# An attention-and-MLP block with gradients on one core: score matmuls of four heads on four 32-row strips from query chunk 1 on

## The chip, the core and the metric

The kernel runs on one core of a Trainium2 chip. The metric is the device time of one execution in microseconds (us); of several executions the median is given. Five engines work side by side: TensorE (PE in the profile, with its weight loads as PEld), VectorE (DVE), ScalarE (ACT), GpSimd (POOL) and SyncE (SP), which here only issues DMAs. TensorE writes into PSUM, which is handed out in banks of 128x512 f32.

## The reference

One adaLN block, forward and backward. 2048 tokens, width D = 512, 32 heads of 16 (DH), MLP width F = 1792:

```python
sa, ca, ga, sb, cb, gb = (silu(c) @ w_mod).reshape(6, D)
h = layernorm(x) * (1 + ca) + sa
q, k, v = heads(h @ wqkv)
p = softmax(q @ k.T * DH**-0.5)
x1 = x + ga * ((p @ v) @ wo)
h = layernorm(x1) * (1 + cb) + sb
out = x1 + gb * (relu(h @ w1 + b1)**2 @ w2 + b2)
```

The outputs are `out` and the gradients of all inputs for a given `grad_out`. Everything is bf16 in memory.

## The kernel before

The attention forward runs in `phase_fwd`. The 2048 queries are cut into 4 chunks (qc) of 512, the 32 heads into 8 groups (g) of four, and each group into two pairs (jp). A unit is one (qc, g, jp); in each unit a loop runs over 16 blocks (kb) of 128 keys. For one kb of one unit there are:

- two score matmuls (L388, 128x512) into the two banks of a tile `st`. The keys KTq hold four heads in four strips of 32 rows (16 rows of a head, the rest zero). Each matmul contracts over all 128 rows, and the queries `QTm0` to `QTm3` are zero outside the strip of their head, so one head's scores come out;
- one exponential on ScalarE over both (L391, 128x1024) into `pu`;
- eight value matmuls (L322, 128x17: 16 values and a column of ones that gives the softmax sum), which accumulate over kb in `accbank`, some blocks later. They wait in a list, `pend`, and a plan with a budget (SPAN, PVT) says how many go out in a block;
- `bg.step(1.14)`: a generator hands out a matmul or so of background work, which is the preparation of weights (`gen_weights`) and the MLP forward and part of the backward of the chunk before (`gen_mlp`: `x1`, `fc1`, `du`, `dx`, `fc2` and the output projection's gradient `gen_do`).

At a unit's end DVE normalises (L329 reciprocal, L330 multiply). `take_o` casts a finished chunk's output to bf16 and sends it through a DMA that transposes it for `gen_mlp`. Loads of the next unit's queries and of the next group's keys (`load_q`, `load_k`) stand on POOL's queue, at kb 1. PSUM's eight banks are: `st` 2 tiles of 2 banks, `accbank` 2, and `mps` 2 for the background. Within this code the orders on the engines TensorE, DVE, ScalarE and SP are written out by hand in chunk 0; from chunk 1 on TensorE and SP follow the order of the code, and a scheduler orders the rest.

Chunk 3 has no later forward to hide its MLP in: `last_chunk` does it after the last exponential (x1 at L817 and L818, layer norm L819 to L824, transposes `turn` L782 and L783, first matmul of fc1 at L838). There the rest of the background (`fc2` of chunk 2, L1255 to L1260) goes between these steps (`bg.take`, `bg.drain`). The attention backward, phase 5 of the trace (L1459 to L1659), is the longest part and isn't touched by the change.

Of the kernel before, what the change touches and what calls it, by code (L numbers as in the profile page):

```python
# [35 lines left out]
class Background:  # L36
# [27 lines left out]
    def step(self, rate):  # L64
# [4 lines left out]
        while self.gens and self.credit > 0:  # L69
# [36 lines left out]
class K:  # L106
# [22 lines left out]
    def dram(self, name, shape, dtype):  # L129
        if name in self.dbg:  # L130
            ap = self.dbg[name]
            assert tuple(ap.shape) == tuple(shape), (name, ap.shape, shape)
            return ap
        return self.dram_pool.tile(list(shape), dtype, name=name)

    def build(self, ctx: ExitStack):
        tc, nc = self.tc, self.nc
# [129 lines left out]
    def phase_fwd(self):  # L267
# [98 lines left out]
        late, self.late = self.late, None  # L366
        bg.until(-1)
        KT = self.KT_next
        for n, (qc, g, jp) in list(enumerate(order))[2:]:
            if (qc, g, jp) == (1, 0, 0):  # L370
                bg.drain()
                es.close()
                self.close_qkv()
                self.open_mlp()
                bg.add(self.gen_weights())
            accb = accp.tile([P, 512], F32, name="accbank")
            acc = accb[:, 0:8 * (DH + 1)].rearrange("p (a s e) -> p a s e", a=2, s=4)
            self.cur_g = g
            for kb in range(ST):
                if kb == (5 if qc == 0 and jp == 1 else 1) and n + 1 < len(order):  # L380
                    if n < 2 * NQ - 1 and jp == 1:
                        bg.until(g + 1)
                    load_q(*order[n + 1])
                    if jp == 1:
                        KTn = load_k(*order[n + 1][:2])
                stt = stp.tile([P, 2, 512], F32, name="st")
                for a in range(2):
                    nc.tensor.matmul(stt[:, a, :], lhsT=KT[:, kb * P:(kb + 1) * P], rhs=QTm[2 * jp + a][:],  # L388
                                     start=True, stop=True)
                pu = pup.tile([P, 2, 512], BF16, name="pu")  # L390
                nc.scalar.activation(pu[:], stt[:], ACT.Exp, scale=self.scale)  # L391
                u = (n, qc, g, jp, kb, acc, pu)
                now = n * ST + kb
                pend.extend((u, a, sub) for a in range(2) for sub in range(4))
                if late:
                    late.pop(0)()
                rate = 1.14 if qc else 1.2
                room = int((SPAN - 2 - bg.plan(rate)) / PVT)
                while pend:
                    age = now - max(pend[0][0][0] * ST + pend[0][0][4], 2 * ST - 2)  # L400
                    if age < 2 or (room <= 0 and age < 4):
                        break
                    pv(pend.pop(0))
                    room -= 1
                bg.step(rate)
            if jp == 1 and n + 1 < len(order):
# [12 lines left out]
        while pend:  # L419
            pv(pend.pop(0))  # L420
# [3 lines left out]
        self.last_chunk(bg, O_b, x0s, O32)  # L424

    def gen_open(self, Vaug, KT, QTm, QTo, stp, bg):

# [334 lines left out]
    def last_chunk(self, bg, O_b, x0s, o32):  # L762
# [51 lines left out]
        for k in range(4):  # L814
# [306 lines left out]
    def gen_weights_1(self):  # L1121
# [46 lines left out]
    def gen_mlp(self, sc, O_b):  # L1168
# [16 lines left out]
        for k in range(4):  # L1185
            x0 = mk.tile([P, D], BF16, name="x0", bufs=2)
            nc.gpsimd.dma_start(x0[:], x_v[:, k, :])
            pt = mps.tile([P, 512], F32, name="pps")
            for kt in range(DT):
                nc.tensor.matmul(pt[:], lhsT=OT[:, k, kt, :], rhs=self.wo[:, kt, :], start=(kt == 0), stop=(kt == DT - 1))  # L1190
# [18 lines left out]
        for ft in range(FT):  # L1209
            pt = mps.tile([P, 512], F32, name="pps")  # L1210
            for kt in range(DT):
                nc.tensor.matmul(pt[:], lhsT=self.w1[:, kt, ft * P:(ft + 1) * P], rhs=xhT[:, :, kt, :],
                                 start=(kt == 0), stop=(kt == DT - 1))
                yield 1
            nc.vector.tensor_scalar(rT[:, ft, :], pt[:], self.bias1[:, ft:ft + 1], 0.0, ALU.add, ALU.max)
# [4 lines left out]
        for ft in range(FT):  # L1220
            pt = mps.tile([P, 512], F32, name="pps")
            for kt in range(DT):
                nc.tensor.matmul(pt[:], lhsT=self.W2gbT[:, ft, kt, :], rhs=gT[:, kt, :], start=(kt == 0), stop=(kt == DT - 1))
# [8 lines left out]
        for k in range(4):  # L1232
# [1 line left out]
            nc.gpsimd.dma_start(gt[:], g_v[:, k, :])  # L1234
            pt = mps.tile([P, 512], F32, name="pps")
            for ft in range(FT):
                nc.tensor.matmul(pt[:], lhsT=duT[:, ft, k * P:(k + 1) * P], rhs=self.W1mT[:, :, ft, :],  # L1237
                                 start=(ft == 0), stop=(ft == FT - 1))
                yield 1
            dx1 = mk.tile([P, D], F32, name="dx1")  # L1240
# [6 lines left out]
            dxT = mk.tile([P, DT, P], BF16, name="dxT", bufs=2)  # L1247
            nc.sync.dma_start_transpose(dxT[:], dxb[:])
            todo.append((k, dxT))
            if k:  # L1250
                yield from self.gen_do(sc, *todo.pop(0))
        def fc2(k):
            pt = mps.tile([P, 512], F32, name="pps")
            for ft in range(FT):
                nc.tensor.matmul(pt[:], lhsT=rT[:, ft, k * P:(k + 1) * P], rhs=self.w2[:, ft, :], start=(ft == 0), stop=False)  # L1255
                yield 1
            nc.tensor.matmul(pt[:], lhsT=self.ones_b[0:1, :], rhs=self.b2gb_b[0:1, :], start=False, stop=True)
            yield 1
            o = mk.tile([P, D], BF16, name="o0", bufs=2)
            nc.vector.tensor_tensor(o[:], pt[:], x1[:, k, :], ALU.add)  # L1260
# [28 lines left out]
    def gen_do(self, sc, k, dxT, pads=None, o32=None):  # L1289
# [6 lines left out]
            nc.gpsimd.dma_start(o32, self.O32_d.rearrange("(st p) d -> p st d", p=P)[:, st, :])  # L1296
        pt = self.mps.tile([P, 512], F32, name="pps")
        for kt in range(DT):
            nc.tensor.matmul(pt[:], lhsT=dxT[:, kt, :], rhs=self.wogaT[:, :, kt, :], start=(kt == 0), stop=(kt == DT - 1))
# [666 lines left out]
```

## Time and profile before

| what | value |
|---|---|
| median of 3 executions | 2506.12 us (2504.64 to 2511.49) |
| span of the profiled execution | 2498.5 us, 7.6 us under the median of the timed runs |
| first exponential of chunk 1 starts | 272.24 us |
| last exponential of the forward ends | 980.54 us |
| first matmul of chunk 3's fc1 (L838) | 998.06 us |
| PE, ACT, DVE, POOL busy over the span | 96%, 91%, 68%, 30% |
| granted TensorE clock | 0.998 |

The span is the time from the first to the last instruction of the profiled execution; that execution has no other time of its own in what is shown, so all differences below are differences of spans. In a row of the timeline stand the start, the time from the first start to the last end of a run of like instructions, the engine, line, operation, tiles and the count (x), and in brackets how long the engine was idle before and what ended it. In a row of groups stand the count, the busy time, the mean time of one, and the idle time before them.

### The profile page before, as it was taken

The numbers are of one execution on the slowest core, as the hardware profiler recorded it, in microseconds if no ns is written. First come the engines' busy times: TensorE is split into PE (matmuls) and PEld (weight loads), VectorE is DVE, ScalarE is ACT, GpSimd is POOL, SyncE is SP. The second block draws the span as 40 slices with busy tenths as digits, with TensorE's granted clock in tenths as the row PEclk, the third lists the DMA queues.
The fourth block names the chain that finished last, engine by engine and source line by source line (L and its number), as shares of the span: only waits on it lengthen the run. The fifth ranks groups of instructions, "written<-read, shape, count | busy, mean of one in ns | idle before, by whom it ended". The sixth has DMA issues, their size and how long they took to land.

```text
span 2498.5 us, 67897 instructions
## 1 busy us (share of the span) xinstructions
PE 2410.2 (96%) x26211; PEld 1061.6 (42%) x26439; DVE 1695.0 (68%) x3487; ACT 2283.1 (91%) x3757; POOL 753.5 (30%) x1337
## 2 busy tenths in 40 slices
PE   8999999999999999999999999999999999999998
PEld 4555555555555555583233332333333333333343
DVE  6222322422332343576999999999999999999957
ACT  7999999999999997534999999999999999999945
POOL 2344531220131022245222323322333222322223
PEclk9999999999999999999999999999999999999999
DMA  4589661541243045499999999999999999999997
GB/s 166 135 179 208 169 125 47 132 100 40 92 114 98 23 123 147 110 199 216 232 235 233 232 227 231 237 234 231 230 235 239 234 230 236 234 233 236 238 217 192
DMA packets 1293547, 454.13 MB, mean 182 GB/s; under 512 B 1236948, under 2 KB 1261398, under 8 KB 1293222
## 3 DMA queue, kind: packets, MB, share of 16 engines
q1 hardware_dynamic: 1252422, 344.68, 71.8%
q0 software_dynamic: 38720, 104.04, 13.9%
q8 instruction: 207, 3.39, 0.6%
q10 hardware_dynamic: 2080, 1.05, 0.2%
q14 instruction: 118, 0.97, 0.1%
HBM read 75.83 MB, written 64.49 MB: 56 GB/s over the span
## 4 chain that ended last, share of the span: by engine, by line
PE 49%; ACT 35%; DMA 7%; issue 5%; DVE 3%; POOL 1%; SPq 1%; ACTq 0%; DVEq 0%; POOLq 0%
ACT pu L391 26%; PE st L1608 17%; PE acckv L1459 8%; ACT pu L1611 6%; DMA dsT<-ds 5%; PE accq L1484 5%; PE st L388 4%; PE dp L1522 2%; PE accbank L322 2%; PE dps L1050 2%; PE dp L1659 1%; PE st L1754 1%; ACT csq L1540 1%; PE pps L1237 1%; DVE ds L1526 1%
## 5 line engine op out<-in xcount | busy, mean ns | idle before, releaser
L1526 DVE TENSOR_TENSOR ds<-dp,pu 128x512 bf16<-128x512 f32 x1888 | 1166.0, 682 | 34.6 <-PE dp L1522 19.1
L1611 ACT ACTIVATE pu<-st 128x512 bf16<-128x512 f32 x2048 | 1073.8, 666 | 34.7 <-PE st L1608 21.3
L391 ACT ACTIVATE pu<-st 128x1024 bf16<-128x1024 f32 x992 | 912.1, 1077 | 4.2 <-PE st L388 3.7
L388 PE MATMUL st<-QTm,KTq 128*128 128x512 bf16 x1859 | 560.9, 377 | 27.1 <-ACT pu L391 6.1
L322 PEld LDWEIGHTS <-pu 128*128 128x128 bf16 x8192 | 346.7, 96 | 236.1 <-issue 3.0
L1522 PE MATMUL dp<-kvm,q 64*128 64x512 bf16 x1024 | 365.0, 384 | 2.0 <-DVE ds L1526 0.7
L322 PE MATMUL accbank<-Vaug,pu 128*128 128x17 bf16 x8192 | 357.4, 171 | 8.3 <-ACT Vaug L522 1.1
L1522 PE MATMUL dp<-kvm,dOTg 64*128 64x512 bf16 x1024 | 363.6, 383 | 0.3
L1608 PE MATMUL st<-kvm,q 64*128 64x512 bf16 x1024 | 349.4, 382 | 5.4 <-ACT pu L1611 0.2
L1608 PE MATMUL st<-kvm,QTg 64*128 64x512 bf16 x1024 | 348.1, 381 | 6.5
L1541 POOL TENSOR_TENSOR ds<-csq,pu 128x512 bf16<-128x512 f32 x128 | 147.2, 1150 | 627.0 <-ACT csq L1540 553.6
L388 PEld LDWEIGHTS <-KTq 128*128 128x128 bf16 x1984 | 188.4, 96 | 176.9 <-issue 124.8
L1459 PE MATMUL acckv<-ds,Qg 128*16 128x512 bf16 x1024 | 176.2, 382 | 0.3
L1459 PE MATMUL acckv<-pu,q 128*16 128x512 bf16 x1024 | 176.3, 383 | 0.0
L1459 PE MATMUL acckv<-ds,q 128*16 128x512 bf16 x1024 | 176.2, 383 | 0.0
L1459 PE MATMUL acckv<-pu,dOg 128*16 128x512 bf16 x1024 | 176.0, 382 | 0.0
L302 POOL DMA_DIRECT2D QTm<-QTq_d x124 | 63.1, 511 | 341.5 <-PE st L388 320.0
L1608 PEld LDWEIGHTS <-q 64*128 64x128 bf16 x1024 | 67.0, 94 | 163.5 <-issue 150.6
L1608 PEld LDWEIGHTS <-QTg 64*128 64x128 bf16 x1024 | 67.1, 94 | 160.6 <-issue 145.7
L329 DVE RECIPROCAL rl<-accbank 128x4 f32<-128x4 f32 x128 | 22.9, 179 | 158.3 <-PE accbank L322 158.2
L1522 PEld LDWEIGHTS <-q 64*128 64x128 bf16 x1024 | 88.8, 93 | 52.9 <-issue 43.3
L1522 PEld LDWEIGHTS <-dOTg 64*128 64x128 bf16 x1024 | 88.2, 93 | 52.9 <-issue 43.8
(390 smaller groups left out, 3055.1 us busy)
## 6 DMA issues: line engine op xcount, KB each, us to landing
KTq<-KTq_d POOLq DMA_DIRECT2D x24, 512.0 KB, 3.9
duT_d<-auT POOLq DMA_DIRECT2D x3, 1792.0 KB, 7.9
aT_d<-rT POOLq DMA_DIRECT2D x3, 1792.0 KB, 11.5
KTq_d<-KTq SPq DMA_DIRECT2D x32, 128.0 KB, 2.1
QTq_d<-ev_fm SPq DMA_DIRECT2D x32, 128.0 KB, 4.3
ktm_d<-ev_tm POOLq DMA_DIRECT2D x32, 128.0 KB, 2.5
VTq_d<-vT POOLq DMA_DIRECT2D x4, 1024.0 KB, 6.3
dx<-dx_d SPq DMA_DIRECT2D x16, 256.0 KB, 4.6
```

The lines of the kernel that those rows point to most:

```text
L302: nc.gpsimd.dma_start(QTm[j][32 * j:32 * j + 32, :], self.QTq_d[g, 32 * j:32 * j + 32, 512 * qc:512 * (qc + 1)])
L322: nc.tensor.matmul(acc[:, a, sub, :], lhsT=pu[:, a, sub * P:(sub + 1) * P], rhs=Vaug[:, kb, h, :], start=(kb == 0 and a == 0 and sub == 0) ...
L388: nc.tensor.matmul(stt[:, a, :], lhsT=KT[:, kb * P:(kb + 1) * P], rhs=QTm[2 * jp + a][:], start=True, stop=True)
L391: nc.scalar.activation(pu[:], stt[:], ACT.Exp, scale=self.scale)
L1050: nc.tensor.matmul(pt[:], lhsT=a[st], rhs=g_tm[:, st, :], start=(st == 0), stop=(st == ST - 1))
L1459: nc.tensor.matmul(acckv[r:r + DH, :], lhsT=T[n][:, ib, col:col + DH], rhs=src[:, a, :], start=(ib == 0), stop=(ib == ST - 1))
L1484: nc.tensor.matmul(accq[r:r + 32, o:o + 256], lhsT=T["K"][:, 4 * c + sub, col:col + 32], rhs=v[:, r // 32 % 2 * 2:r // 32 % 2 * 2 + 2, 4 * ...
L1522: nc.tensor.matmul(dp[:], lhsT=T["dOT"][rd, ib * P:(ib + 1) * P], rhs=masked["VT"][a][rd, 512 * c:512 * (c + 1)], start=True, stop=True)
L1526: nc.vector.tensor_tensor(dsg[:, i, a], dp[:], pu[:, a, :], ALU.mult)
L1541: nc.gpsimd.tensor_tensor(dsg[:, i, 1], f[:], pu[:, 1, :], ALU.mult)
L1608: nc.tensor.matmul(stt[:], lhsT=T["QT"][rs, q], rhs=masked["KT"][a][rs, c0:c0 + 512], start=True, stop=True)
L1611: nc.scalar.activation(pu[:, a, :], stt[:], ACT.Exp, scale=self.scale)
```

## The change

Chunk 0 stays as it is. From chunk 1 on the forward is a new function, `fwd_rest`:

- A unit is a group of four heads (24 units of 16 kb). For each kb there are four score matmuls of 32 rows each (L503, `KT[r]` and `QTm[r]` of strip r), into two tiles `st` (A for heads 0 and 1, B for heads 2 and 3), two exponentials (L507) as large as before, and 16 value matmuls (L482), half of them ahead of the background and half behind it, for the block before.
- The queries are loaded once for a group, unmasked (`load_group_fwd`).
- `bg.burst(3.0, self, most)` hands out up to four background matmuls in a row (L158, the helper `mm`), and stops behind a matmul that ends an accumulation. What is missing to four is filled up with matmuls whose result is never read (L520, 128 rows, into the tile A of the next kb, 760 of them over chunks 1 to 3).
- `st` gets 3 tiles of 2 banks, `accbank` 1 bank (two before), `mps` 1 bank (two before). Since there is one `accbank`, at kb 1 of a group the value matmuls are held back until DVE has normalised the group before; kb 2 then does two blocks.
- One reciprocal (128x16) and one multiply (128x256) normalise a group.
- Between the chunks 0 and 1 the pools of PSUM are closed and opened anew.
- `fc2` of chunk 2 is no longer handed out in the forward beyond its first 128 tokens. Behind the last exponential the background has 45 matmuls in place of 24, through one bank (`m2`); the x1 matmuls get two banks of their own (`m3`). From fc1 of chunk 3 on the order of all engines is that of before.

```diff
+    def burst(self, rate, k, most=4):
+        n = 0
+        if self.hold > 0:
+            self.hold -= 2
+            return n
+        self.credit = min(self.credit + rate, 4.0)
+        while self.gens and self.credit > 0 and n < most:
+            k.stopped = False
+            r = self.next()
+            ...
+            n += r
+            if k.stopped:
+                break
+        return n
...
+        bg.drain()
+        es.close()
+        self.close_qkv()
+        self.open_mlp()
+        bg.add(self.gen_weights())
+        while pend:
+            pv(pend.pop(0))
+        self.fwd_rest(bg, KT, kp, pup, QTm, Vaug, O32)
...
+    def fwd_rest(self, bg, KT, kp, pup, QTm, Vaug, O32):
+        for name in ("fwacc", "fwst", "mps"):
+            self.close_pool(name)
+        self.mps = self.open_pool("mps", bufs=1, space=PSUM)
+        stp = self.open_pool("fwst", bufs=3, space=PSUM)
+        accp = self.open_pool("fwacc", bufs=1, space=PSUM)
+        ...
+        for n, (qc, g) in enumerate(groups):
+            for kb in range(ST):
+                if kb == 1 and n + 1 < len(groups):
+                    KTn = self.load_group_fwd(*groups[n + 1], kp, QTm)
+                tiles = tiles or [stp.tile([P, 2, 512], F32, name="st") for _ in range(2)]
+                for h in range(4):
+                    r = slice(32 * h, 32 * h + 32)
+                    nc.tensor.matmul(tiles[h // 2][:, h % 2, :], lhsT=KT[r, kb * P:(kb + 1) * P], rhs=QTm[g % 2][r, :],
+                                     start=True, stop=True)
+                pus = [pup.tile([P, 2, 512], BF16, name="pu") for _ in range(2)]
+                for t, pu in zip(tiles, pus):
+                    nc.scalar.activation(pu[:], t[:], ACT.Exp, scale=self.scale)
+                held = kb == 1 and n > 0
+                while len(pend) > 1 and not held:
+                    pv(pend.pop(0))
+                most = 5 if held else 2 if kb == 2 and n > 0 else 4
+                done = 0 if qc == SC - 1 and f"fc2_{SC - 2}" in bg.seen else bg.burst(3.0, self, most)
+                if pend and not held:
+                    pv(pend.pop(0))
+                pend += [((qc, g, kb, pus), half) for half in range(2)]
+                ...
+                    tiles = [stp.tile([P, 2, 512], F32, name="st") for _ in range(2)]
+                    for _ in range(int(most - done)):
+                        nc.tensor.matmul(tiles[0][:, 0, :], lhsT=KT[:, 0:P], rhs=QTm[g % 2][:], start=True, stop=True)
...
-        mps = self.mps = Pools(m2, m2, self.open_pool("mps2", bufs=1, space=PSUM))
+        m3 = self.open_pool("mps2", bufs=2, space=PSUM)
+        mps = self.mps = Pools(m3, m3)
...
         bg.drain()
+        mps.pools = (m3, m3, m2)
```

Every background matmul goes through the new helper `mm`, which notes whether it ended an accumulation, and `gen_mlp` waits two steps longer behind each `dx`.

TensorE in the middle of chunk 2 before, one kb (`W2gbT` and `fT` are background, `pu` are exponentials of earlier blocks):

```order
L388 MATMUL st_11315<-QTm2_142,KTq_10725 128x512 [waits Activation_49]
...
L388 MATMUL st_11315<-QTm3_143,KTq_10725 128x512
...
L322 MATMUL accbank_11201<-Vaug_123,pu_11257 128x17
...
L322 MATMUL accbank_11201<-Vaug_123,pu_11273 128x17
...
L1223 MATMUL pps_11331<-fT_9510,W2gbT_4907 128x512 [waits DVE_49]
L388 LDWEIGHTS KTq_10725
L388 MATMUL st_11333<-QTm2_142,KTq_10725 128x512 [waits Activation_49]
```

And the same stretch after, one kb of four heads:

```order
L520 MATMUL st_11537<-QTm0_140,KTq_10780 128x512 [waits PE_49]
...
L503 MATMUL st_11537<-QTm0_140,KTq_10780 128x512
...
L503 MATMUL st_11538<-QTm0_140,KTq_10780 128x512 [waits Activation_49]
...
L482 LDWEIGHTS pu_11516
L482 MATMUL accbank_11313<-Vaug_123,pu_11516 128x17
...
L158 MATMUL pps_11560<-fT_9926,W2gbT_4906 128x512 [waits DVE_49]
...
L482 LDWEIGHTS pu_11517 [waits Activation_49]
L482 MATMUL accbank_11313<-Vaug_123,pu_11517 128x17
```

What moved: the scores of two exponentials go out in one go, the second tile's waiting for the exponential that frees it, and the background stands in one block between two lots of eight value matmuls.

TensorE where chunk 1 begins, after (L347 is the value matmul of chunk 0; before, the value matmuls of that last unit followed later, among those of chunk 1):

```order
L347 LDWEIGHTS pu_4870 [waits Activation_49]
L347 MATMUL accbank_4629<-Vaug_123,pu_4870 128x17
...
L503 LDWEIGHTS KTq_4721 [waits DMASW2_49,DVE_49,DMASW3_49]
L503 MATMUL st_4952<-QTm0_140,KTq_4721 128x512 [waits PE_49]
...
L503 MATMUL st_4953<-QTm0_140,KTq_4721 128x512
L520 LDWEIGHTS KTq_4721
L520 MATMUL st_4973<-QTm0_140,KTq_4721 128x512
```

What moved: all value matmuls of chunk 0 now stand ahead of the first scores of chunk 1, and these wait for DVE, whose last reader of the old `accbank` frees the banks.

DVE behind the last exponential, before (`o0` reads the bank of one `fc2` and frees it, `x1_l` that of x1; `stats`, `mv`, `ve` and `nmr` are the layer norm):

```order
L1260 TENSOR_TENSOR o0_17230<-pps_17050,x1_13625 128x512
L818 TENSOR_TENSOR x1_l_17192<-pps_17241,x0_17131 128x512
...
L818 TENSOR_TENSOR x1_l_17192<-pps_17285,xh2_17189 128x512
L823 SCALAR_TENSOR_TENSOR nmr_17240<-mv_17237,rstd2_17239 128x1
L819 BN_STATS stats_17236<-x1_l_17192 128x6
L820 BN_AGGR mv_17237<-stats_17236 128x2
...
L1260 TENSOR_TENSOR o0_17312<-pps_17233,x1_13625 128x512
L783 COPY fT_17315<-tp_17322 128x512
```

And after:

```order
L918 TENSOR_TENSOR x1_l_17697<-pps_17787,xh2_17694 128x512
L923 SCALAR_TENSOR_TENSOR nmr_17742<-mv_17739,rstd2_17741 128x1
L921 TENSOR_SCALAR ve_17740<-mv_17739 128x1
L919 BN_STATS stats_17738<-x1_l_17697 128x6
L923 SCALAR_TENSOR_TENSOR nmr_17742<-mv_17739,rstd2_17741 128x1
L1362 TENSOR_TENSOR o0_17806<-pps_17703,x1_14054 128x512
L920 BN_AGGR mv_17739<-stats_17738 128x2
...
L1362 TENSOR_TENSOR o0_17825<-pps_17809,x1_14054 128x512
L1362 TENSOR_TENSOR o0_17844<-pps_17828,x1_14054 128x512
```

What moved: three evictions of `fc2` stand there in place of two, the first of them behind the last x1; TensorE's 15 matmuls of the next `fc2` (`pps_17809`) and of the one after wait for the eviction before them, since they share a bank.

More of the change, by code (lines that the diff above doesn't have):

```diff
@@ L134, in dram, with mm @@
         return self.dram_pool.tile(list(shape), dtype, name=name)
+    def mm(self, out, stop, **kw):
+        self.nc.tensor.matmul(out, stop=stop, **kw)
+        self.stopped = stop
     def build(self, ctx: ExitStack):
@@ L368, in phase_fwd @@
         KT = self.KT_next
+        order = order[:2 * NQ]
         for n, (qc, g, jp) in list(enumerate(order))[2:]:
[L370 to L375, printed above, removed]
             accb = accp.tile([P, 512], F32, name="accbank")
@@ L379, in phase_fwd @@
             for kb in range(ST):
-                if kb == (5 if qc == 0 and jp == 1 else 1) and n + 1 < len(order):
+                if kb == 5 and n + 1 == len(order):
+                    KTn = self.load_group_fwd(1, 0, kp, QTm)
+                elif kb == (5 if jp == 1 else 1) and n + 1 < len(order):
                     if n < 2 * NQ - 1 and jp == 1:
@@ L405, in phase_fwd @@
                 bg.step(rate)
-            if jp == 1 and n + 1 < len(order):
+            if jp == 1:
                 if n < 2 * NQ - 1:
@@ L424, in phase_fwd, with load_group_fwd, pv @@
         self.last_chunk(bg, O_b, x0s, O32)
+    def load_group_fwd(self, qc, g, kp, QTm):
+        t = kp.tile([P, self.S], BF16, name="KTq")
+        with self.tc.high_priority():
+            self.nc.gpsimd.dma_start(QTm[g % 2][:], self.QTq_d[g, :, 512 * qc:512 * (qc + 1)])
+            self.nc.gpsimd.dma_start(t[:], self.KTq_d[g])
+        return t
+    def fwd_rest(self, bg, KT, kp, pup, QTm, Vaug, O32):
+        nc, NQ, ST, SC = self.nc, self.NQ, self.ST, self.SC
+        for name in ("fwacc", "fwst", "mps"):
[3 more added lines that the diff above has]
+        accp = self.open_pool("fwacc", bufs=1, space=PSUM)
+        groups = [(qc, g) for qc in range(1, SC) for g in range(NQ)]
+        acc = None
+        def pv(w):
+            nonlocal acc
+            ((qc, g, kb, pus), half) = w
+            if kb == 0 and half == 0:
+                accb = accp.tile([P, 512], F32, name="accbank")
+                acc = accb[:, 0:16 * (DH + 1)].rearrange("p (a s e) -> p a s e", a=4, s=4)
+            for a in range(2):
+                j = 2 * half + a
+                for sub in range(4):
+                    nc.tensor.matmul(acc[:, j, sub, :], lhsT=pus[half][:, a, sub * P:(sub + 1) * P], rhs=Vaug[:, kb, 4 * g + j, :],
+                                     start=(kb == 0 and j == 0 and sub == 0), stop=False, skip_group_check=True)
+            if kb < ST - 1 or half == 0:
+                return
+            st0 = 4 * qc
+            rl = self.rl[:, st0:st0 + 4, 4 * g:4 * g + 4].rearrange("p s a -> p a s")
+            nc.vector.reciprocal(rl, acc[:, :, :, DH])
+            o = O32[:, :, 4 * g * DH:4 * (g + 1) * DH].rearrange("p s (a d) -> p a s d", a=4)
+            nc.vector.tensor_tensor(o, acc[:, :, :, 0:DH], rl.unsqueeze(3).to_broadcast([P, 4, 4, DH]), ALU.mult)
+            if g == NQ - 1 and qc < SC - 1:
+                bg.add(self.gen_mlp(qc, self.take_o(qc, O32)))
+        pend = []
+        tiles = None
+        for n, (qc, g) in enumerate(groups):
[18 more added lines that the diff above has]
+                pend += [((qc, g, kb, pus), half) for half in range(2)]
+                tiles = None
+                if (n, kb) != (len(groups) - 1, ST - 1):
+                    tiles = [stp.tile([P, 2, 512], F32, name="st") for _ in range(2)]
+                    for _ in range(int(most - done)):
+                        nc.tensor.matmul(tiles[0][:, 0, :], lhsT=KT[:, 0:P], rhs=QTm[g % 2][:], start=True, stop=True)
+            KT = KTn
+        while pend:
+            pv(pend.pop(0))
@@ L1249, in gen_mlp @@
             todo.append((k, dxT))
+            yield ("wait", 2)
             if k:
@@ L1254, in fc2 @@
             for ft in range(FT):
-                nc.tensor.matmul(pt[:], lhsT=rT[:, ft, k * P:(k + 1) * P], rhs=self.w2[:, ft, :], start=(ft == 0), stop=False)
+                self.mm(pt[:], lhsT=rT[:, ft, k * P:(k + 1) * P], rhs=self.w2[:, ft, :], start=(ft == 0), stop=False)
                 yield 1
-            nc.tensor.matmul(pt[:], lhsT=self.ones_b[0:1, :], rhs=self.b2gb_b[0:1, :], start=False, stop=True)
+            self.mm(pt[:], lhsT=self.ones_b[0:1, :], rhs=self.b2gb_b[0:1, :], start=False, stop=True)
             yield 1
@@ L1298, in gen_do @@
         for kt in range(DT):
[L1299 removed]
+            self.mm(pt[:], lhsT=dxT[:, kt, :], rhs=self.wogaT[:, :, kt, :], start=(kt == 0), stop=(kt == DT - 1))
             yield 1
```

18 lines of the change are left out of this document (11 added, 7 removed).

## The prediction

> **What bounds the kernel now.** I read the page first, then the forward of chunks 1 to 3 in three windows, then the groups and the timeline of ScalarE, then TensorE's neighbours in one block of keys.
>
> ```profile
> span 2498.5 us, 67897 instructions
> PE 2410.2 (96%) x26211; PEld 1061.6 (42%) x26439; DVE 1695.0 (68%) x3487; ACT 2283.1 (91%) x3757; POOL 753.5 (30%) x1337
> ...
> L391 ACT ACTIVATE pu<-st 128x1024 bf16<-128x1024 f32 x992 | 912.1, 1077 | 4.2 <-PE st L388 3.7
> ```
>
> Averages over the span say that TensorE is the busiest. The stage that the change touches says otherwise:
>
> ```profile
> core 0: us, PE busy (x) PEld busy (x) DVE busy (x) ACT busy (x) POOL busy (x), PEclk, DMA share, GB/s
> 272.24:508.80 236.56, 223.57 (x2774) 127.94 (x2826) 77.93 (x221) 234.64 (x257) 71.60 (x98) 1.00 0.47 112
> 508.80:744.60 235.80, 229.22 (x2783) 129.03 (x2834) 73.44 (x222) 235.72 (x257) 48.76 (x83) 1.00 0.33 86
> 744.60:980.60 236.00, 228.63 (x2790) 128.84 (x2840) 76.37 (x222) 235.33 (x257) 46.81 (x81) 1.00 0.33 88
> 980.60:998.06 17.46, 14.38 (x90) 6.86 (x92) 11.45 (x34) 5.48 (x8) 4.12 (x7) 1.00 0.76 256
> ```
>
> ScalarE is busy for 705.69 of 708.36 us. The fourth line is the stretch from the last exponential to chunk 3's fc1, which I call the tail. Whether ScalarE could be quicker is seen in its timeline, here four exponentials one by one, a run of 48, and the stage's group with its first and last rows:
>
> ```profile
> 514.04 1.02 ACT L391 ACTIVATE pu<-st 128x1024 bf16<-128x1024 f32 x1
> 514.97 1.02 ACT L391 ACTIVATE pu<-st 128x1024 bf16<-128x1024 f32 x1
> 515.87 1.03 ACT L391 ACTIVATE pu<-st 128x1024 bf16<-128x1024 f32 x1
> 516.77 1.04 ACT L391 ACTIVATE pu<-st 128x1024 bf16<-128x1024 f32 x1
> ...
> 598.63 44.17 ACT L391 ACTIVATE pu<-st 128x1024 bf16<-128x1024 f32 x48
> ```
> ```profile
> L391 ACT ACTIVATE pu<-st 128x1024 bf16<-128x1024 f32 x769 | 706.6, 1083 | 2.6 <-PE st L388 2.4
> ```
> ```profile
> 272.24 1.09 ACT L391 ACTIVATE pu<-st 128x1024 bf16<-128x1024 f32 x1
> ...
> 975.85 4.68 ACT L391 ACTIVATE pu<-st 128x1024 bf16<-128x1024 f32 x5
> ```
>
> Starts come 0.90 us apart, but each lasts 0.01 us longer than the one before it: the ends are 0.91 to 0.92 apart. The run of 48 gives (44.17 - 1.05) / 47 = 0.917 us per exponential. The group counts 769 because the window touches the one before. From 272.24 to 980.54 stand 768 exponentials; 767 x 0.9167 + 1.09 = 704.2 us of the 708.3 are this pitch, and 4.1 us are lost. The largest loss is one stall:
>
> ```profile
> 319.26 0.59 PE L1212 MATMUL pps<-fT,w 128*128 128x512 bf16 x2 [1.89 <-DMA fT<-xh]
> ...
> 320.38 1.02 ACT L391 ACTIVATE pu<-st 128x1024 bf16<-128x1024 f32 x1 [1.82 <-PE st L388]
> ```
>
> So the forward as a stage can give back 4.1 us at most, whatever TensorE does, unless the pitch itself changes.
>
> **The change, part by part.** *Exponentials.* Their count (24 groups x 16 x 2 = 768) and shape stay. Cost: the same pitch.
>
> *TensorE in one block of keys.* Prices come from these rows of before, the last five from the attention backward:
>
> ```profile
> 601.12 0.37 PE L322 MATMUL accbank<-Vaug,pu 128*128 128x17 bf16 x9
> 601.35 0.38 PE L1212 MATMUL pps<-fT,w 128*128 128x512 bf16 x1
> 601.61 0.59 PE L388 MATMUL st<-QTm,KTq 128*128 128x512 bf16 x2
> 602.04 0.38 PE L322 MATMUL accbank<-Vaug,pu 128*128 128x17 bf16 x9
> ```
> ```profile
> 1600.15 0.39 PE L1608 MATMUL st<-kvm,q 64*128 64x512 bf16 x1
> 1600.15 0.39 PE L1522 MATMUL dp<-kvm,q 64*128 64x512 bf16 x1
> 1600.47 0.39 PE L1459 MATMUL acckv<-ds,q 128*16 128x512 bf16 x2
> 1600.48 0.39 PE L1459 MATMUL acckv<-pu,q 128*16 128x512 bf16 x2
> 1600.80 0.39 PE L1608 MATMUL st<-kvm,q 64*128 64x512 bf16 x1
> ```
>
> Two 512-column matmuls take 0.43 us from start to start, so 0.216 each; nine value matmuls 0.23, so 0.0255 each. In the second fence two matmuls on 64-row strips start in the same moment, then four on 16-column strips within 0.01 us, and the next pair comes 0.65 us after the first. Two lots at 0.216 make 0.43; the rest, 0.22, goes for two changes of the strip form, 0.11 each. Before, TensorE needs for two exponentials 4 scores (0.86), 16 value matmuls (0.41) and about 2.3 background matmuls. After, for one block of four heads (two exponentials, 2 x 0.9167 = 1.833 us): the four strips 0.216 if all four run at once, two changes 0.21, 16 value matmuls 0.41, four background or idle matmuls 0.86; sum 1.70. That leaves 0.13 us. At kb 1 of a group (five matmuls, no values) it is 1.51, at kb 2 (two, and 32 values) 1.67. ScalarE would stay the bound and everything here is hidden.
>
> That four 32-row strips run at once no row of before shows. Its bounds: all four at once 0.216 (the four column strips, nearest in number), two at a time 0.43 (the two row strips, nearest in kind), one after another 0.86. I take all four, since in both rows every strip in the array starts together. The limit is 0.216 + 0.13 = 0.35 for the strips; above that TensorE sets the pace.
>
> On this the Trainium skill has a figure, "TensorE: Matmul & The Clock Gate", Part 3: four 32-row matmuls of 512 columns were measured 3.07 times as fast as one after another. By that the strips would take 4 x 0.216 / 3.07 = 0.28 us and the block 1.77, an estimate, still under 1.83, and the sum would be the same. Its page "TensorEngine Tiling (Array Packing)", Key Properties, speaks against the change: a change of the tiling form drains TensorE. The 0.11 us per change above agree with it and are paid in the 1.70.
>
> *Handing over a single background bank and a single value bank.* A background accumulation ends, DVE evicts it, the next one starts in the same bank:
>
> ```profile
> L1215 DVE TENSOR_SCALAR rT<-pps,bias 128x512 bf16<-128x512 f32 x42 | 31.5, 751 | 105.9 <-PE pps L1212 103.5 <-DMA QTm<-QTq_d 2.5
> ```
>
> A burst stops at an accumulation's end, so between it and the next lie eight value matmuls, idle ones, the strips and eight more values: about 1.0 to 1.2 us. DVE needs 0.75 and two hand-overs of some 0.2, so 1.2. TensorE waits at most 0.2 us, once in two or more blocks, and earns 0.13 in each; three `st` tiles keep ScalarE fed meanwhile. Below nothing it can't go, as no rows are quicker. I take 0.3 us in all for the forward (24 normalisations and the three starts of a chunk), with 0 to 4 as ends. The loads (POOL) go out a whole group, 29 us, ahead, longer than the unit of 14.7 before; nothing waits for them. The stall at 319.26 goes: by the order at least seven blocks (12.8 us) lie between the last of `x1` and the first of `fc1`, for a DMA that was 1.89 us late. I give the whole 4.1 us back: **-4.1** (ends 0 and -4.1).
>
> *Between chunks 0 and 1.* PSUM's pools are opened anew, so the first scores wait until DVE has read the last `accbank`. Before, the tail shows exactly such a step:
>
> ```profile
> 980.59 0.36 PE L322 MATMUL accbank<-Vaug,pu 128*128 128x17 bf16 x8 [0.33 <-ACT pu L391]
> 980.99 0.18 DVE L329 RECIPROCAL rl<-accbank 128x4 f32<-128x4 f32 x1 [5.97 <-PE accbank L322]
> ...
> 981.56 0.23 DVE L330 TENSOR_TENSOR O<-accbank,rl 128x64 f32<-128x64 f32 x1
> ```
>
> The last exponential ended at 980.54; DVE was done at 981.79, 1.25 later. Then 0.05 to TensorE, a change of form 0.1, the scores 0.39 (as a row of them lasts) and 0.1 to ScalarE: an idle ScalarE of **+1.9** where it had none. Ends: 1.25 (TensorE's part already under way) and 2.5.
>
> *The tail.* Before it takes 17.5 us, and its DVE and TensorE rows are
>
> ```profile
> 991.98 0.68 DVE L818 TENSOR_TENSOR x_l<-pps,xh 128x512 f32<-128x512 f32 x1
> ...
> 992.19 1.89 PE L1255 MATMUL pps<-w,rT 128*128 128x512 bf16 x8
> ...
> 992.79 0.68 DVE L819 BATCH_NORM_STATS2 stats<-x_l 128x6 f32<-128x512 f32 x1
> ...
> 994.02 0.38 PE L1257 MATMUL pps<-b2gb_b,ones_b 1*128 1x512 bf16 x1
> 994.33 0.62 PE L782 MATMUL tp<-ident,xh 128*128 128x128 bf16 x8
> ...
> 994.62 0.69 DVE L1260 TENSOR_TENSOR o<-pps,x 128x512 bf16<-128x512 f32 x1
> ...
> 998.06 1.25 PE L838 MATMUL pps<-fT,w 128*128 128x512 bf16 x5 [0.52 <-DVE fT L783]
> ```
>
> TensorE works through it nearly without a pause (14.38 of 17.46 us), and 21 more `fc2` matmuls (45 instead of 24) go into its row: 21 x 0.216 = 4.5 us at least. To that come waits. The 45 are three accumulations in one bank. The first ends some 0.75 us earlier than in this trace the x1 steps allow (x1 has its two banks). Its eviction stands on DVE behind the last x1 and its statistics, whose rows end at 993.47; less 0.75 and with 0.7 for itself that is about 993.5. From there 15 matmuls (3.24), the eviction between (0.60 from the last matmul's start to DVE's, as 994.02 to 994.62; 0.69; 0.05 back; less 0.22 already counted: 1.1), 15 more (3.24): 1001.1. The transposes and copies from 994.33 to 998.06 took 3.7 us, of which some 0.8 was ScalarE's last `xh` coming late, which will be ready by then: about 1004.0, so the tail is **+6.0**. Ends: +4.5 (no waits) and +7.5 (0.75 not gained, the transposes at 3.7).
>
> From fc1 on all orders are as before, and nothing waits for something older than the tail: the rest costs nothing.
>
> *Sum*: -4.1 + 0.3 + 1.9 + 6.0 = +4.1 us on the span, 2502.6. The median of the timed runs stands 7.6 us above the profiled span; I put the difference on the median: 2506.1 + 4.1 = 2510.2, say 2510.
>
> **Rivals.** *A, slower: the strips go two at a time,* as the 64-row pair does in the only rows of this kind. Then a block needs 1.70 + 0.22 = 1.92 us, 0.08 over 1.833; 384 blocks x 0.08 = 31 us, and with -4.1 no longer given back about 2540. It decides where the strips pass 0.35 us. One after another would be 1.70 + 0.65 = 2.35, 384 x 0.52 = 198 us, 2705. For it: no row shows four row strips. Against it: the four column strips.
>
> *B, slower by a few more: waits on the single banks.* Some 130 background accumulations end in the stage's 384 blocks, one in three; the slack between two is 3 x 0.13 = 0.39 us. Were TensorE to wait 0.5 us at each, 130 x 0.11 = 14 us would come on top: 2524; it decides at 0.39. For it: DVE has no second bank to drain. Against it: three score tiles and DVE busy only a third of the stage.
>
> *C, quicker: the tail's additions hide and the forward gains more.* Were the tail's 21 matmuls to fit into its 3.1 us of pauses and the lost 4.1 come back, it would be 2506.1 - 4.1 + 1.9 + 1.4 = 2505, no change. It is quicker than 2498.6 only if the pitch of the exponentials falls: were it the 0.903 of their starts, 767 x 0.0137 = 10.5 us, 2500 with the tail as above and 2495 with a hidden one. Against it: in the run of 48 the backlog is there all the time and the pitch is 0.917.
>
> **How the numbers follow.** About 0.3% (7.5 us) is what a measurement of this kernel can tell from no change: 2498.6 to 2513.6. The forecast's own sum, between its ends: -4.1 + 0 + 1.25 + 4.5 = +1.7 and 0 + 4 + 2.5 + 7.5 = +14, so 2508 to 2520, which I give 0.55, of which a fifth lies above 2513.6. A gets 0.13, B 0.12, the no-change form of C 0.10, its quicker form 0.10. Faster 0.10; same 0.44 + 0.10 = 0.54; slower 0.11 + 0.13 + 0.12 = 0.36. The range leaves out most of A and half of the quicker form of C: 2499 to 2528.
>
> **What would show it.** The exponentials at a pitch of 0.917 with no gap near 319 and one of about 1.9 us at the first of chunk 1, and the same again from first to last near 704 us: the forward's terms. Four score rows (L503) starting within some 0.01 us: the strips; starts 0.2 us apart in pairs would be A, with ScalarE idle before each exponential on PE. Waits of the background matmuls (L158) on DVE that carry over to ScalarE's idle time would be B. The first fc1 23 to 24 us after the last exponential: the tail. I am wrong if the rows of the backward change, too.

## The result, and the profile after

| kernel | executions | median us (lowest to highest) | ratio to before, 95% interval |
|---|---|---|---|
| after, as first measured | 4 | 2524.3 (2515.3 to 2527.3); before 2507.1 | 1.0062 [1.0041, 1.0083] |
| after, measured again | 11 | 2520.6 (2511.9 to 2530.6); before 2506.0 | 1.0060 [1.0040, 1.0079] |
| before against itself | 12 | 2508.7 (2502.2 to 2515.6); before 2506.5 | 1.0007 [0.9993, 1.0021] |

The change costs 0.6%, about 15 us, where +4 was forecast. The page and the windows after, the stage again in three parts and then the tail:

```profile
span 2525.3 us, 69141 instructions
...
L507 ACT ACTIVATE pu<-st 128x1024 bf16<-128x1024 f32 x768 | 704.9, 1127 | 6.0 <-PE st L503 5.6
```
```profile
core 0: us, PE busy (x) PEld busy (x) DVE busy (x) ACT busy (x) POOL busy (x), PEclk, DMA share, GB/s
275.11:511.40 236.29, 226.09 (x3013) 114.93 (x3055) 64.45 (x149) 232.49 (x253) 52.34 (x64) 0.99 0.42 104
511.40:747.70 236.30, 228.94 (x3042) 118.76 (x3087) 78.91 (x194) 236.24 (x259) 38.35 (x64) 1.00 0.36 89
747.70:984.08 236.38, 228.14 (x3034) 118.05 (x3076) 70.27 (x173) 236.22 (x258) 36.20 (x59) 1.00 0.36 89
984.08:1008.51 24.43, 20.24 (x111) 9.78 (x113) 12.03 (x33) 5.59 (x8) 4.71 (x8) 0.93 0.55 188
```

ScalarE is busy for nearly all of the second and third window (236.24 of 236.30 us and 236.22 of 236.38): it is still the bound, and all but 0.2 us of its idle time lies in the first. Its timeline gives the places:

```profile
275.11 1.94 ACT L507 ACTIVATE pu<-st 128x1024 bf16<-128x1024 f32 x2 [2.01 <-PE st L503]
277.44 18.44 ACT L507 ACTIVATE pu<-st 128x1024 bf16<-128x1024 f32 x20 [0.39 <-PE st L503]
...
346.05 1.94 ACT L507 ACTIVATE pu<-st 128x1024 bf16<-128x1024 f32 x2 [2.23 <-PE st L503]
349.00 596.32 ACT L507 ACTIVATE pu<-st 128x1024 bf16<-128x1024 f32 x650 [1.01 <-PE st L503]
```

The run of 650 gives (596.32 - 1.1) / 649 = 0.917 us, the pitch of before. The wait of 2.01 us is the opening of the pools. The ones of 2.23 and 1.01 us are new, and these rows tell where from, first POOL before the change, then POOL and TensorE after it:

```profile
312.03 5.22 POOL L1137 TENSOR_SCALAR w<-w,opcbT 128x1792 bf16<-128x1792 bf16 x3
...
318.32 1.76 POOL L1137 TENSOR_SCALAR w<-w,opcbT 128x1792 bf16<-128x1792 bf16 x1
```
```profile
326.80 10.12 POOL L1251 TENSOR_TENSOR w<-w,mod 128x512 bf16<-128x512 bf16 x9 [11.30 <-DMA w<-in_B_w_dram]
...
338.03 6.96 POOL L1238 TENSOR_SCALAR w<-w,opcbT 128x1792 bf16<-128x1792 bf16 x4
```
```profile
343.31 0.39 PE L158 MATMUL pps<-fT,w 128*128 128x512 bf16 x1 [0.80 <-POOL w L1238]
...
345.05 0.39 PE L158 MATMUL pps<-fT,w 128*128 128x512 bf16 x1 [1.34 <-POOL w L1238]
```

The first fc1 of chunk 1 needs w1 scaled by POOL (L1238). In POOL's order those four instructions now stand behind nine multiplications of w2 (L1251), which waited 11.30 us for a DMA; before, they stood ahead of them (L1137, from 312.03 on). TensorE waits in the middle of a burst, with the next scores behind it. Behind these two waits its granted clock was 0.50 from 347 to 349 us, and there the idle time of 1.01 us falls.

The tail, TensorE's rows with their waits for DVE's evictions (L1362):

```profile
996.03 0.39 PE L158 MATMUL pps<-b2gb_b,ones_b 1*128 1x512 bf16 x1
997.69 3.18 PE L158 MATMUL pps<-w,rT 128*128 128x512 bf16 x14 [1.27 <-DVE o L1362]
1000.80 0.39 PE L158 MATMUL pps<-b2gb_b,ones_b 1*128 1x512 bf16 x1
1001.97 3.18 PE L158 MATMUL pps<-w,rT 128*128 128x512 bf16 x14 [0.78 <-DVE o L1362]
...
1008.51 0.82 PE L939 MATMUL pps<-fT,w 128*128 128x512 bf16 x3 [0.52 <-DVE fT L883]
```
```profile
984.10:988.00 3.90, 3.44 (x21) 1.97 (x23) 2.54 (x7) 0.05 (x1) 0.76 (x1) 0.56 0.48 160
```

From the last exponential (984.07) to fc1 it takes 24.4 us, against 17.5. The two waits for the single bank stand there, 1.27 and 0.78 us, and TensorE's granted clock was 0.56 in the tail's first 3.9 us. So fc1 begins 10.5 us later than before; a second profile says 9.7. Of the 10.5, 2.9 are there at the first exponential of chunk 1 (275.11 against 272.24; 1.5 in the second profile), 0.7 come in the stretch of the exponentials, 6.9 in the tail.

### The profile page after: what moved, and what is told of

The parts are those of the page before. It is cut to its first block, busy times and chain, and to the rows that moved or that the text cites. A ratio compares the mean times of both kernels' runs of the same rounds, so it can differ in the third digit from the quotient of the medians.

```text
span 2525.3 us, 69141 instructions
## 1 busy us (share of the span) xinstructions
PE 2424.0 (96%) x26994; PEld 1032.7 (41%) x27199; DVE 1683.0 (67%) x3343; ACT 2283.0 (90%) x3757; POOL 715.7 (28%) x1265
## 4 chain that ended last, share of the span: by engine, by line
PE 40%; ACT 8%; DMA 8%; issue 2%; DVE 2%; POOL 0%; SPq 0%; DVEq 0%; ACTq 0%; POOLq 0%
PE st L1710 16%; PE acckv L1561 8%; ACT pu L1713 6%; PE accq L1586 5%; DMA dsT<-ds 4%; PE dps L1151 2%; PE dp L1624 2%; DMA keep<-ds 1%; DMA dqT<-dq_t 1%; ACT csq L1642 1%; PE st L1856 1%; DVE ds L1628 1%; PE dp L1761 1%; PE st L1667 1%; PE st L1574 1%
## 5 line engine op out<-in xcount | busy, mean ns | idle before, releaser
L507 ACT ACTIVATE pu<-st 128x1024 bf16<-128x1024 f32 x768 | 704.9, 1127 | 6.0 <-PE st L503 5.6
L482 PEld LDWEIGHTS <-pu 128*128 128x128 bf16 x6144 | 216.5, 96 | 158.0 <-issue 83.2
L482 PE MATMUL accbank<-Vaug,pu 128*128 128x17 bf16 x6144 | 265.2, 172 | 10.1 <-ACT pu L507 7.4
L520 PE MATMUL st<-QTm,KTq 128*128 128x512 bf16 x670 | 202.7, 379 | 6.3 <-ACT pu L507 2.7
L503 PE MATMUL st<-QTm,KTq 32*128 32x512 bf16 x1536 | 171.9, 385 | 5.2 <-issue 1.0
L410 PE MATMUL st<-QTm,KTq 128*128 128x512 bf16 x435 | 130.0, 377 | 10.1 <-ACT pu L413 4.0
L347 PEld LDWEIGHTS <-pu 128*128 128x128 bf16 x2048 | 86.4, 96 | 59.6 <-issue 3.0
```

Of the source, the lines that this page charges most:

```text
L482: nc.tensor.matmul(acc[:, j, sub, :], lhsT=pus[half][:, a, sub * P:(sub + 1) * P], rhs=Vaug[:, kb, 4 * g + j, :], start=(kb == 0 and j == ...
L503: nc.tensor.matmul(tiles[h // 2][:, h % 2, :], lhsT=KT[r, kb * P:(kb + 1) * P], rhs=QTm[g % 2][r, :], start=True, stop=True)
L507: nc.scalar.activation(pu[:], t[:], ACT.Exp, scale=self.scale)
L520: nc.tensor.matmul(tiles[0][:, 0, :], lhsT=KT[:, 0:P], rhs=QTm[g % 2][:], start=True, stop=True)
```

## The experiments

The second measurement of the kernel after:

> The changed kernel as it is, a second time, for a second profile and more runs. Theory: all of its loss arises before chunk 3's fc1 (first row 10.5 us later than before in the profile); the backward from there on has the same orders, and its 16 us in that profile are scatter. Then the ratio comes out at 1.003 to 1.006, and the stretch from the first fc1 to the end nearer to the 1500 us of before than the 1517 of the first profile. Rival: the backward itself is slower, by another placement of buffers. Then the ratio stays at 1.006 or above and the stretch at 1510 to 1520 us again.

The ratio, 1.0060, lies at the upper end of the theory's range, and the stretch from fc1 to the end of the span was 1517.9 us, not nearer to 1500: both are what the rival named. Of the 15 us, 10 are explained by fc1; the rest is taken up below, with the kernel before run against itself.

**The tail.** Two kernels. The first goes on handing out the background:

```diff
-                done = 0 if qc == SC - 1 and f"fc2_{SC - 2}" in bg.seen else bg.burst(3.0, self, most)
+                done = bg.burst(3.0, self, most)
```

> The background goes on being handed out at the end of chunk 3's forward, so that 11 of its matmuls in place of 45 stand behind the last exponential. Theory (TensorE's work and the single bank set the tail's length): 34 x 0.216 = 7.3 us and two evictions of about 1 us less, tail 24.4 to about 15 to 16 us, time 8 to 9 us under the changed kernel, ratio to before about 1.002. Rival (the chain from x1 through the layer norm to the transposes sets it, the matmuls only fill): the tail stays above 17.5 us, and the gain is under 7 us. A second rival: the forward has no room for 34 more and the last exponential comes later by what the tail gives.

Ratio 1.0018 [1.0003, 1.0033]. The last exponential ended at 983.30 us as in the second profile of after (983.25), so the 34 matmuls cost the forward nothing, and 30 of them took places of unread ones (27169 weight loads in the trace, 27199 after). The tail fell from 24.5 to 16.8 us, 7.7: more than the 34 x 0.216, less than the theory's 8.4 to 9.4. Some 1.3 us of the 7.7 belong to the clock and not to the matmuls: it was 1.00 in the tail's first 3.9 us, and what that is worth the run on the stall shows below. Near its new end it is the chain that sets the time, as the rival had it:

```profile
993.86 0.40 PE L882 MATMUL tp<-ident,xh 128*128 128x128 bf16 x4 [0.48 <-ACT xh L924]
996.00 0.48 PE L882 MATMUL tp<-ident,xh 128*128 128x128 bf16 x4 [1.75 <-ACT xh L924]
...
1000.14 1.04 PE L939 MATMUL pps<-fT,w 128*128 128x512 bf16 x4 [0.52 <-DVE fT L883]
```

The transposes wait for ScalarE's xh. With 24 matmuls (before) the tail was 17.5 us, with 11 it is 16.8: so most of the first two dozen seem to lie beside the chain. That compares two kernels that differ in more than this count. The second kernel gives fc2 the two x1 banks there:

```diff
...
-            pt = mps.tile([P, 512], F32, name="pps")
+            pt = (self.fc2_pool or mps).tile([P, 512], F32, name="pps")
...
+        self.fc2_pool = m3
         bg.drain()
```

> Behind the last exponential the second and third accumulation of fc2 take the two x1 banks, nothing else changes. Theory (the tail of 24.5 us has 21 matmuls more, 4.5 us, and some 2.4 us of waits for the one bank's eviction): the tail falls to 22 us. Rival (TensorE is busy all the time and the chain to the transposes sets the rest): the tail stays at 24 to 24.5 us.

```profile
999.92 3.20 PE L158 MATMUL pps<-w,rT 128*128 128x512 bf16 x14
...
1006.48 0.82 PE L941 MATMUL pps<-fT,w 128*128 128x512 bf16 x3 [0.52 <-DVE fT L884]
```

The last exponential ended at 984.23, so the tail is 22.25 us: 2.2 less than after, the 1.27 + 0.78 of the waits. Ratio 1.0035 [1.0015, 1.0054]. The theory of the bank holds: 2.2 of the 6.9 us that the tail grew are its waits.

**The stall in chunk 1.**

```diff
-            nc.gpsimd.tensor_scalar(w1[:, kt, :], w1[:, kt, :], self.opcbT[:, kt:kt + 1], 1.0, ALU.mult, ALU.mult)
+            nc.vector.tensor_scalar(w1[:, kt, :], w1[:, kt, :], self.opcbT[:, kt:kt + 1], 1.0, ALU.mult, ALU.mult)
```

> The four scalings of w1 (128x1792) are done by DVE and no longer stand on POOL's queue behind nine multiplications of w2. Theory: the two waits of fc1 on POOL in chunk 1 (0.80 and 1.34 us), the idle ScalarE of 2.23 us after them and that of 1.01 us in the half clock behind go; the stretch from the first to the last exponential falls from 709.0 to 705.5 to 706 us. Rival: something else is late there next (the transposed x, the bias), and the stretch stays above 708 us.

```profile
274.13 20.27 ACT L507 ACTIVATE pu<-st 128x1024 bf16<-128x1024 f32 x22 [1.83 <-PE st L503]
294.56 645.74 ACT L507 ACTIVATE pu<-st 128x1024 bf16<-128x1024 f32 x704 [0.16 <-ACT pu L507]
940.46 38.60 ACT L507 ACTIVATE pu<-st 128x1024 bf16<-128x1024 f32 x42 [0.16 <-ACT pu L507]
```

From 274.13 to 979.06: 704.9 us, even under the 705.5 expected, and within 0.8 of the forecast's floor of 704.2. Nothing else was late. Ratio 1.0030 [1.0017, 1.0044].

This run shows one thing more. Nothing of its tail was changed, yet the tail took 23.15 us, 1.3 less than after. In its first 3.9 us the granted clock was 1.00, where it was 0.56 after:

```profile
979.06:982.96 3.90, 3.00 (x31) 1.81 (x33) 2.71 (x8) 0.62 (x3) 0.76 (x1) 1.00 0.50 159
```

The first x1 matmul began 4.53 us behind the last exponential, after 5.81. The same half clock stood there in the second profile of after (0.56) and in the kernel with two banks (0.56); why not here is open.

**What the unread matmuls do.** The loop that issues L520 is taken out:

```diff
-                    for _ in range(int(most - done)):
-                        nc.tensor.matmul(tiles[0][:, 0, :], lhsT=KT[:, 0:P], rhs=QTm[g % 2][:], start=True, stop=True)
```

> The 760 matmuls whose result is never read are left out, nothing else. Theory: ScalarE's pitch of 0.917 us sets the forward, TensorE has room in any case; the stretch of the exponentials stays at 709 us within 1 us, and the time the same. Rival: with TensorE idle for over half of a block its granted clock falls in the blocks without background, the strips, values and the switch then take twice as long, and the stretch grows by 5 us or more, with a granted clock below 0.95 in a window of the forward.

```profile
273.72:519.50 245.78, 233.37 (x2777) 111.64 (x2784) 66.21 (x152) 234.69 (x255) 53.01 (x65) 0.72 0.41 100
519.50:765.30 245.80, 230.84 (x2830) 115.44 (x2846) 78.17 (x193) 236.84 (x257) 38.69 (x65) 0.85 0.31 85
765.30:1011.00 245.70, 230.65 (x2816) 114.25 (x2829) 70.22 (x173) 237.64 (x258) 35.72 (x59) 0.81 0.32 86
```

The rival was right by far: ratio 1.0161 [1.0135, 1.0188], 25 us slower than the kernel after, the stretch 737.3 us, the granted clock 0.72 to 0.85. One place where the clock falls, with its window:

```profile
381.52 0.39 PE L503 MATMUL st<-QTm,KTq 32*128 32x512 bf16 x2 [0.23 <-ACT pu L507]
381.84 0.36 PE L482 MATMUL accbank<-Vaug,pu 128*128 128x17 bf16 x8
382.44 0.36 PE L482 MATMUL accbank<-Vaug,pu 128*128 128x17 bf16 x8 [0.24 <-ACT pu L507]
382.74 1.23 PE L503 MATMUL st<-QTm,KTq 32*128 32x512 bf16 x4
383.89 0.77 PE L482 MATMUL accbank<-Vaug,pu 128*128 128x17 bf16 x16
```
```profile
382.00:383.00 1.00, 0.76 (x18) 0.47 (x16) 0.00 (x0) 1.00 (x3) 0.00 (x0) 0.92 0.00 0
383.00:384.00 1.00, 0.92 (x8) 0.21 (x5) 0.00 (x0) 1.00 (x3) 0.00 (x0) 0.50 0.06 16
```

A row of four strips lasts 1.23 us in place of 0.39, 16 values 0.77. A block with strips and values alone still fits into 1.83 us; where background comes back, the half clock makes it too long until the clock is up again. The Trainium skill ("TensorE: Matmul & The Clock Gate", Part 1) ties the half clock to an idle window of some 3.4 us, and tells in the same part of a kernel whose clock fell with short idle times between groups of matmuls. Here no such window stands ahead of the fall: the longest idle time that the rows show in the 3.4 us before it is 0.24 us, so the measurement goes against the first. Two short idle times (0.23 and 0.24 us) stand there, and 2.3 us in which strips and values alone ran; which of the two the clock went by, no run here tells.

**TensorE's block.** Two kernels, one execution each. First every exponential takes 256 of the 512 columns of each score bank:

```diff
...
-                    nc.scalar.activation(pu[:], t[:], ACT.Exp, scale=self.scale)
+                    nc.scalar.activation(pu[:, :, 0:256], t[:, :, 0:256], ACT.Exp, scale=self.scale)
```

> From chunk 1 on each exponential covers half of its columns (the other half of pu holds ones), so ScalarE needs about 0.49 us in place of 0.917 and TensorE sets the pace: the pitch of a block of four heads is then TensorE's own price of it. Theory: 1.70 us (strips 0.216, two changes of form 0.21, 16 values 0.41, four long matmuls 0.86), 384 blocks in 653 us and some stalls, 655 to 665 us from the first to the last exponential. Rival A (strips in pairs): 1.92 us, 737 us, but that would have shown in the changed kernel already. Rival (TensorE's real slack is larger): under 1.65 us, below 640 us.

```profile
L510 ACT ACTIVATE pu<-st 128x512 bf16<-128x512 f32 x768 | 416.8, 595 | 270.7 <-PE st L506 270.7
```
```profile
599.92 0.40 PE L506 MATMUL st<-QTm,KTq 32*128 32x512 bf16 x4
600.25 0.36 PE L482 MATMUL accbank<-Vaug,pu 128*128 128x17 bf16 x8
...
601.61 0.40 PE L506 MATMUL st<-QTm,KTq 32*128 32x512 bf16 x4
```

ScalarE now waits for TensorE (270.7 us), and an undisturbed block takes 601.61 - 599.92 = 1.69 us: the forecast's 1.70. From first to last exponential it was 683.6 us, 19 above the range: 384 x 1.70 = 653 and 31 of waits. Of these, 18 are value matmuls that wait for an exponential and 5 are fc1 waiting for w1 on POOL; background matmuls wait 1.9 us for DVE. In the kernel after ScalarE's longer pitch covers most of them. Then the four scores on all 128 rows:

```diff
-                    nc.tensor.matmul(tiles[h // 2][:, h % 2, :], lhsT=KT[r, kb * P:(kb + 1) * P], rhs=QTm[g % 2][r, :],
+                    nc.tensor.matmul(tiles[h // 2][:, h % 2, :], lhsT=KT[:, kb * P:(kb + 1) * P], rhs=QTm[g % 2][:],
```

> The four score matmuls of a block contract over all 128 rows in place of a 32-row strip each (the sum over four heads comes out, which is not the reference's score); all else, idle matmuls too, as in the changed kernel. Theory: strips and two changes of form, 0.43 us, become 4 x 0.216 = 0.86; the block is 2.13 us, over ScalarE's 1.83, and the stretch from the first to the last exponential grows by 384 x 0.30 = 114 us to about 820 us. Rival (the strips are not what makes room): the stretch stays within 20 us of 709.

From 274.64 to 1089.55, 814.9 us, 106 more than after; the block that is there most often, half of all, took 2.13 us, 0.30 over 1.833. The strips are what makes the room, at the price that the sum had.

**The backward's scatter, and the parts together.**

> The kernel before against itself, for the scatter of the ratio and a second profile. Both theories: ratio 1.000 within 0.0015; first exponential of chunk 1 at about 272 us, fc1 at about 998. If the 4 to 6 us by which the changed kernels are slower than their fc1 says are scatter of the backward, its stretch from fc1 to the end should spread here as it does there, from 1497 to about 1515 us; if they are a cost of the change, it stays near 1500.

Its first exponential came at 272.65 and fc1 at 998.04, as in the first profile. The stretch from fc1 to the end of the span was 1510.8 us there and 1500.4 in the first profile of the very same kernel; in the changed ones it was 1499.9 to 1517.9. So 10 us of the 16 that the first profile of after showed behind fc1 are within what one kernel does.

One place sets the kernels apart, though. It is the same matmul in the same order, here before and after:

```profile
2417.81 2.75 PE L1754 MATMUL st<-WmT,dqT 128*128 128x512 bf16 x12
```
```profile
2441.48 4.69 PE L1856 MATMUL st<-WmT,dqT 128*128 128x512 bf16 x12 [7.48 <-DMA dqT<-dq_t]
```

TensorE waits there for a transposing DMA: 7.48 us after, 6.00 in the second profile of after, and 1.6 to 6.3 us in four other changed kernels (two banks in the tail, w1 on DVE, and further down both parts together and the early block). It doesn't wait in the one with fc2 in the forward, nor in the one without unread matmuls, nor in either profile of before. Counted from fc1, the first profile of after is 5.6 us behind that of before ahead of this place, and 15.2 us behind it. So the scatter of before, which arose elsewhere, doesn't prove that the change costs nothing here. The engines' orders are the same from fc1 on; why the DMA is late there is open.

> fc2 handed out in the forward to its end, and w1 scaled by DVE, together. Theory (the gains add up): the exponentials from first to last 705 us, the tail 16.8 us, fc1 at 996 us, 2 us ahead of before; with the part of the backward that isn't explained the ratio to before is 0.999 to 1.002. Rival: with POOL's queue free something of the last chunk is late, or the forward has no room for the 34 matmuls without the stall; then fc1 is at 999 us or later.

fc1 came at 995.6 (exponentials 274.00 to 979.53, tail 16.1 us). Ratio 0.9996 [0.9981, 1.0011]: the gains add up, and the result is as quick as before, not measurably quicker.

Two kernels tried for more. One puts the last chunk's du into the forward:

```diff
...
+        self.du_l = duT = self.ra.tile([P, FT * 512], BF16, name="auT")[:].rearrange("p (f k) -> p f k", f=FT)
+        for ft in range(FT):
+            pt = mps.tile([P, 512], F32, name="pps")
+            for kt in range(DT):
+                self.mm(pt[:], lhsT=self.W2gbT[:, ft, kt, :], rhs=gT[:, kt, :], start=(kt == 0), stop=(kt == DT - 1))
+                yield 1
+            nc.vector.tensor_copy(duT[:, ft, :], pt[:])
...
```

> As the kernel with w1 on DVE, and the 56 du matmuls of the last chunk, which need no attention output, go into places of the forward where a matmul with an unread result stood; 16 fc2 matmuls are left behind the last exponential, and half of the squares between fc1 and dx go from ScalarE to DVE. Theory: fc1 at about 996 us, and 44 matmuls less behind it, 9.5 us, of which ScalarE (14 x 0.69 + 7 x 0.63 = 14.1 us against TensorE's 12.1) gives back 2: 7 to 9 us under before, ratio 0.996 to 0.999 with the unexplained part. Rival: TensorE's pauses in the tail without the early du halve its clock in fc1 and ScalarE sets the pace there, and the ratio is 1.000 or more.

Ratio 0.9995 [0.9973, 1.0016]: the gain of 7 to 9 us did not come. Up to dx the theory held: the row of the first dx came at 1010.76 us against 1019.65 before, 8.9 earlier, even with a halved clock at fc1:

```profile
996.60:1000.00 3.40, 3.33 (x8) 1.19 (x9) 0.70 (x3) 0.69 (x1) 0.00 (x0) 0.50 0.00 0
...
1010.76 6.21 PE L958 MATMUL pps<-W1mT,auT 128*128 128x512 bf16 x28
```

At the same instruction of the backward near 1221 us it was 7.5 ahead, near 1885 us 3.8, near 2264 us 4.5 behind. Where it went is not settled; the untouched backward alone scatters by 10 us. The other kernel takes away the wait at chunk 1's start:

```diff
+        first = []
+        for i in range(2):
+            t = stp.tile([P, 2, 512], F32, name="st")
+            ...
+            nc.scalar.activation(pu[:], t[:], ACT.Exp, scale=self.scale)
+            first.append(pu)
         while pend:
             pv(pend.pop(0))
...
```

> As the kernel with fc2 in the forward and w1 on DVE; besides, the scores and exponentials of chunk 1's first block go out in the old PSUM tiles before the values of chunk 0 are finished. Theory: the idle ScalarE of 2.0 us at the start of chunk 1 falls to 0.2 us or less, the last exponential and fc1 come 1.8 us earlier (978 and 994 us), the ratio to before is 0.998 to 1.0. Rival: the next scores wait as long for the old banks, only later, and fc1 stays at 995.6.

```profile
272.19 2.01 ACT L444 ACTIVATE pu<-st 128x1024 bf16<-128x1024 f32 x2
...
276.78 1.94 ACT L519 ACTIVATE pu<-st 128x1024 bf16<-128x1024 f32 x2 [2.58 <-PE st L515]
```

The first block came 1.8 us earlier, but ScalarE then idled for 2.58 us in the next: the rival, and 2 us worse than it, as fc1 was at 997.7 and not at 995.6. Ratio 0.9991 [0.9975, 1.0007].

## Why the prediction was right or wrong

The measured time, 15 us over before, lies inside the stated range, but at the upper end of the forecast's own sum (+1.7 to +14) and above it. The range reached further up for the sake of rival A, which did not come. So that it held is in part luck: one term failed, one was too small, and part of the excess is unexplained.

- *The bound.* Right. The pitch stayed at 0.917 us over 650 exponentials, and with the stall gone the stretch is 704.9 us, as the floor of 704.2 said. Rival C's quicker pitch did not come.
- *TensorE's block.* Right: 1.69 us measured against 1.70. With short exponentials the four strips start within 0.013 us of each other in all 384 blocks, so all four run at once and rival A was wrong. In the kernel after, the second pair starts 0.06 to 0.33 us behind the first in 143 of 384 blocks; each time that is 0.05 us behind the end of an exponential, the one that frees its tile, so it is a wait and not A's price. Of the sum's terms the strips with their changes of form were tested: 128-row scores made the block 2.13 us, 0.43 more, as the sum says.
- *The 4.1 us to be given back.* This step failed. The stall at 319 went, as forecast, but a new one of 3.2 us took its place at 343: fc1's wait for w1 on POOL's queue, behind w2's multiplications. The sum checked the loads on that queue, not the order of its scalings. With them on DVE, the stretch fell by 4.0 us, so this step alone is 4 of the 11 us by which the sum was short.
- *The pools.* +1.9 forecast, 2.01 measured (1.87 in the second profile).
- *Single banks in the forward.* 0.3 us forecast; there is no ScalarE wait there that a bank explains. Rival B did not come, and its waits are hardly there: the background matmuls wait 1.4 us for DVE in the whole stage after, and 1.9 us with short exponentials, where B needed 0.5 us at each of 130 accumulations.
- *The tail.* +6.0 forecast, +6.9 measured. What the sum lacked is the clock. At full clock (w1 on DVE) the tail was 23.15 us, 5.6 over before, and x1 began 4.53 us behind the last exponential where it was 5.22: the 0.75 us that the sum put down to x1's two banks are there, but for 0.06. At half clock in the first 3.9 us x1 began at 5.81, and the tail took 1.3 us more. The bank's waits cost 2.2, as TensorE without them showed.
- *The rest, "costs nothing".* Open. fc1 comes 10 us later, by two profiles, and the time is 15 us longer, with an interval whose lower end is 10. In the six other changed kernels that were timed and leave the part behind fc1 as it is in the change, the time differs from what fc1 says by -1.9 to +3.4 us, within the interval or at its edge. One kernel alone scatters by 10 us in the backward. Against scatter alone speaks the wait for the transposing DMA, which six of eight profiles with this backward order and a changed forward show and neither of before. Whether 3 to 5 us belong to the change, these runs don't tell.

## What to carry to other kernels

Find the floor of the stage first (here the number of exponentials times their pitch): a change that frees another engine can give back only the time above it, and pays for what it moves behind the stage. When work moves in time, look through every engine's queue for what it will meet there, small preparing instructions included. Room made on TensorE may have to be filled, even with unread matmuls: left empty here, it was paid for in clock (0.72 to 0.85) and 25 us.

## What the runs showed of the hardware

- TensorE's clock was halved with no pause longer than 0.24 us in the 3.4 us ahead of it; in the last 2.3 us of these, strips and 17-column matmuls alone ran (granted clock 0.50 from 383 us on without the unread matmuls).
- Four matmuls of 512 columns on four 32-row strips start within 0.013 us of each other in all 384 blocks with short exponentials; on all 128 rows in place of the strips, the block took 2.13 us and not 1.70.
- Two executions of the same kernel differ by 10 us in a stage of 1500 us (1500.4 and 1510.8), without a difference in instructions.
